# Threshold attention and hash-routed experts: moving GpSimd's scatters and early gathers between the steps of a head pair, and thinning the copies behind the experts' transfers

## The chip, the core and the metric

The kernel runs on one core of a Trainium2 chip. The metric is the device time of one execution in microseconds (us), the median of three runs. A core has five engines that run their own instruction queues side by side and wait for each other through semaphores: TensorE (PE, matrix products and transposes), VectorE (DVE), ScalarE (ACT), GpSimd (POOL) and SyncE (SP, which here only issues DMA transfers). GpSimd issues the indirect transfers, those in which a list of indices says which rows go where.

## The reference

Two blocks follow each other. The first is attention with a threshold: 8 batches, 8 heads, 576 tokens, head size 64, in float32.

```python
scores = scale * np.matmul(q, k.transpose(0, 1, 3, 2))
thresh = np.max(scores, axis=-1, keepdims=True) - tau
scores = np.where(scores >= thresh, scores, -1000000000.0)
scores = scores - np.max(scores, axis=-1, keepdims=True)
attn = np.exp(scores)
attn = attn / (np.sum(attn, axis=-1, keepdims=True) + 1e-09)
return np.matmul(attn, v).astype(np.float32)
```

Its output, brought to 4608 rows of 512 numbers, goes through one of 8 experts for each row. A hash of the token's id picks the expert.

```python
expert_idx = token_ids * np.int64(2654435761) % np.int64(E)
for e in range(E):
    mask = expert_idx == e
    xe = x[mask]
    h = np.maximum(xe @ w1[e], 0.0)
    out[mask] = h @ w2[e]
```

w1 takes a row from 512 to 1024 numbers, w2 back to 512.

## The kernel before

**Attention** is cut into 32 head pairs p: two heads of one batch, and the batch runs fastest, so that pairs 8·hp to 8·hp + 7 belong to heads 2·hp and 2·hp + 1. A pair has five steps, numbered s = 0 to 4. Step 0 takes the last 64 queries of both heads together; steps 1 to 4 take 128 queries of each head. The loop counts steps through with n = 5p + s, from 0 to 165, and LAST = 160 is the first step past the last pair. The order of all instructions in this loop is written out by hand, and each engine executes its own in this order.

One step's work passes through the engines like this:

- `score` (L235, PE) writes the scores of the next step into PSUM, in a buffer `sc`.
- `negate` (L246, DVE) copies them out negated, as `ns`, and keeps the row's extreme. After the last head of the step GpSimd adds the threshold to it (L253, `thr`).
- `expo` (L260, ACT) takes the exponential into `w`.
- `mask` (L271, DVE), one step later, sets what lies under the threshold to zero, for which it needs `thr`, and sums the row.
- `turn_w` (L282, PE), two steps later, transposes the weights into a PSUM buffer `tr`. There is one such buffer. `put_wT` (L298 and L303, ACT) copies it out to `wT_a` or `wT_b`, and only then can the next transposes begin.
- `av_part` (L313, PE) multiplies the transposed weights with v. `put_oT` (L329, ACT) copies the products out, `turn_o` (L282, PE, written to `av`) transposes them back.
- `add_eps` (L343, GpSimd, in step 1 of the next pair) and the reciprocal (L740, DVE, in step 2, ahead of that step's negations) prepare the divisor `rec` from the row sums.
- `put_xm` (L352, DVE, in step 0 two pairs later) divides, and SyncE stores the result to `x_scratch` in DRAM: one transfer at L358 and two at L363.
- `scale_k` (L215, GpSimd) scales the keys of the next pair, in step 1.

**Routing** goes on beside this, in small pieces. The tokens' slots are computed early. Then `scatters` gives one piece a call: 36 times an indirect transfer of 128 token numbers to the table of slots (L542), then some empty pieces, then the loads of the table into `sidx`, `stok` and `stok_odd`, and at last the indices of the first expert's rows, `gidx_0`. The loop takes one piece at the end of each of the steps 0, 2, 3 and 4.

**Early gathers**: of the first expert's rows 5 times 128 are needed, each in four parts of 128 columns (one part for each of the four groups of heads). Three of the four parts are complete before attention ends, so 15 pieces can be fetched in it: `fetch_early` (gather at L119 from `x_scratch` into `xg`) fetches one of them if n is over G0 and pieces are left. It is called at the start of each step 0 and at the end of each of the steps 3 and 4; with G0 = 130 the first is at n = 133 and the last at n = 155, which is step 0 of pair 31. All gathers read the tensor to which `put_xm` writes.

**The experts** follow, each with rows gathered (`fetch`, L119), transposed, multiplied with w1 and w2 and scattered to the output (`put_squares`, L1042). While one expert is multiplied, the rows of another come in and those of a third go out. Behind each of these indirect transfers stands `pause`, which copies one index table over another that is no longer used (L1027, 128 partitions by 152 numbers), twice; this takes place 157 times in the kernel: behind the 127 scatters of `put_squares` for the experts but the last and behind the 30 gathers of `fetch` for the experts from 2 on. The scatters of the last expert have no `pause`.

Of the kernel before, what the change touches and what calls it, by code (L numbers as in the profile page):

```python
# [20 lines left out]
def kernel(  # L21
# [12 lines left out]
    nc = tc.nc  # L34

    B, H, D, S = qT.shape
    N, DIN = out.shape
    E, _, F = w1.shape
    P = 128
    HP = H // 2  # L40
# [10 lines left out]
    NS = 5  # L51
# [47 lines left out]
    stok = consts.tile([P, E, NB], I32, name="stok")  # L99
    stok_odd = consts.tile([P, E, NB], I32, name="stok_odd")  # L100
# [23 lines left out]
    def fetch_0(kt, hp):  # L124
        gather(x_rows, xg_bufs[kt][:, P * hp:P * hp + P], gidx_0[:, kt, hp:hp + 1])
# [18 lines left out]
    with tc.tile_pool(name="a_q", bufs=1) as a_q, \  # L144
# [73 lines left out]
        def heads(n):  # L218
            return 1 if n % NS == 0 else 2
# [317 lines left out]
        placed, routed = [], []  # L537
# [130 lines left out]


        LAST = NS * NP  # L670
        G0 = NS * ((HP - 1) * B + 2)
        early = [(kt, hp) for kt in range(KT) for hp in range(HP - 1)]
        pieces, scatter_pieces = route(), scatters()
        h_pieces, held, LATE = early_h(), {}, (0, 6, 1, 7, 2, 3, 4, 5)
# [2 lines left out]
        def fetch_early(n):  # L677


            if n > G0 and early:  # L680
                assert routed
                fetch_0(*early.pop(0))

        def fill(n):
            for _ in range(n):
                next(h_pieces, None)

        with tc.manual_schedule():
            make_identity(nc, ident[:])

            tr = ps_tr.tile([P, 2, 512], FP32, name="tr")
            for _ in range(17):
                nc.tensor.transpose(tr[:, 0, 0:P], ident[:], ident[:])
            nc.gpsimd.dma_start(out=tau_in[:],
                                in_=bass.AP(tensor=tau.tensor, offset=0, ap=[[0, P], [1, 1]]))

            nc.vector.tensor_scalar(out=k_scale[:], in0=tau_in[:], scalar1=0.0, scalar2=SCALE,
                                    op0=ALU.is_ge, op1=ALU.mult)  # L700
            nc.vector.tensor_scalar(out=kts[0][:, 0], in0=kts[0][:, 0], scalar1=k_scale[:],
                                    scalar2=None, op0=ALU.mult)
            nc.scalar.activation(kts[0][:, 1], kts[0][:, 1], AF.Copy, scale=k_scale[:])
            nc.vector.tensor_scalar(out=drop[:], in0=tau_in[:], scalar1=0.0, scalar2=3e38,
                                    op0=ALU.is_lt, op1=ALU.mult)
            nc.vector.tensor_tensor(out=drop[:], in0=drop[:], in1=tau_in[:], op=ALU.max)
            constants()
            next(pieces)
            score(0, 0)
            for n in range(LAST + NS + 1):  # L710
                p, s = divmod(n, NS)
                m = n - 2
                if s == 0:
                    fetch_early(n)
                if s == 0 and p + 2 < NP:
                    load_pair(p + 2)
                if s == 0 and p + 1 < NP:
                    load_v(p + 1)
                if s == 2 and p in (20, 24):
                    load_w1(p // 4 - 5)  # L720
                if s == 2 and p in (22, 26):
                    load_w2((p - 22) // 4)

                if (s == 3 and p > 0 or s == 2 and p in (9, 11, 13)) and not placed:
                    next(pieces)
                if s == 1 and 3 <= p < 2 + KT:
                    nc.sync.dma_start(out=xg_bufs[p - 2][:], in_=xg_bufs[0][:])

                if s == 1 and 2 + KT <= p < 2 + KT + N // DIN:
                    r0 = DIN * (p - 2 - KT)  # L730
                    nc.sync.dma_start(
                        out=x_dram[r0:r0 + DIN, DIN - P:].rearrange("(t p) m -> p t m", p=P),
                        in_=xg_bufs[0][:].rearrange("p (t m) -> p t m", m=P))
                q = p - 1
                if s == 1 and 0 <= q < NP:
                    add_eps(q)
                if s == (1 if p else 3) and p + 1 < NP:
                    scale_k(p + 1)
                if s == 2 and 0 <= q < NP:
                    nc.vector.reciprocal(recs[q][:], recs[q][:])  # L740
                if n == LAST + NS:
                    fill(2)
                if s == 0 and p >= 2:
                    turn_o()
                if n == LAST:
                    for k in (0, 2):
                        tr = ps_sc.tile([P, 2, 512], FP32, name="sc")
                        early_xT(tr, k, k + 2, 0, CO - 1)
                if s in (1, 2) and 0 <= q < NP and n != LAST + 1:
                    av_part(q, 0, ((0, 1, 2), (3, 4))[s - 1])  # L750
                if n < LAST and s in (1, 2):
                    negate(n, 0)
                    expo(n, 0)
                if s == 2 and 0 <= q < NP:
                    put_oT(0)
                if n > LAST:
                    fill(1)
                turned = 0 <= m < LAST
                if turned:
                    tr = turn_w(m, 0)  # L760
                    put_wT(m, 0, tr)
                if n == LAST:
                    put_xm(p - 2)
                    av_part(q, 0, (0, 1, 2))
                if n >= LAST:
                    fill(1)
                if n == LAST:
                    tr = ps_sc.tile([P, 2, 512], FP32, name="sc")
                    early_xT(tr, 4, 5, 0, CO - 1)
                if s in (3, 4) and 0 <= q < NP:  # L770
                    av_part(q, 1, ((0, 1, 2), (3, 4))[s - 3])
                if n < LAST and s not in (1, 2):
                    negate(n, 0)
                    expo(n, 0)
                if s == 0 and p > 0 and not placed:
                    next(pieces)
                if s == 0 and p >= 2 and n != LAST:
                    put_xm(p - 2)
                if s == 4 and 0 <= q < NP:
                    put_oT(1)  # L780
                if s in (3, 4) and turned:
                    tr = turn_w(m, 1)
                if n + 1 < LAST:
                    score(n + 1, 0)
                if s == 4 and turned:
                    put_wT(m, 1, tr)
                if n < LAST and heads(n) == 2:
                    negate(n, 1)
                    expo(n, 1)
                if s == 3 and turned:  # L790
                    put_wT(m, 1, tr)
                if n + 1 < LAST:
                    score(n + 1, 1)
                if s in (0, 1) and turned:
                    tr = turn_w(m, 1)
                    put_wT(m, 1, tr)
                if 0 < n <= LAST:
                    for j in range(heads(n - 1)):
                        mask(n - 1, j)
                if s != 1 and placed:  # L800
                    next(scatter_pieces, None)
                if s > 2:
                    fetch_early(n)
                if n == LAST:
                    fill(1)
            assert not early
            nc.vector.tensor_tensor(out=stok[:], in0=stok[:], in1=stok_odd[:], op=ALU.min)
            for h in range(4):
                rows, n = slice(32 * h, 32 * h + 32), (NB - h + 3) // 4
                nc.vector.tensor_copy(gidx[rows, 0:n], stok[rows, E - 1, h::4])  # L810
                nc.vector.tensor_copy(gidx[rows, KT - 1:KT],
                                      stok[rows, E - 1, NB - 4 + h:NB - 3 + h])
            for g in range(4):
                rows, n = slice(32 * g, 32 * g + 32), min(KT, NB - KT * g)
                nc.vector.tensor_copy(gidx_x[rows, 1:, 0:n], stok[rows, 1:, KT * g:KT * g + n])
            for _ in pieces:
                pass
            nc.vector.scalar_tensor_tensor(
                out=qidx[:], in0=stok[:], scalar=4.0,
                in1=quart[:, :, None].to_broadcast([P, E, NB]), op0=ALU.mult, op1=ALU.add)  # L820
            for kt in range(KT):
                fetch_0(kt, HP - 1)
            fill(FO * 2 * (CO - 1) - 18)
            tr = ps_tr.tile([P, 2, 512], FP32, name="tr")
            early_xT(tr, 0, KT, CO - 1, CO)

    with tc.tile_pool(name="m_x", bufs=1) as m_x, \
# [195 lines left out]

        def pause():

            for _ in range(2):
                nc.gpsimd.tensor_copy(stok_odd[:], stok[:])  # L1027

        def put_squares(e, i):

# [174 lines left out]
```

## Time and profile before

| what | us |
|---|---|
| median of three runs (lowest, highest) | 918.26 (918.19, 919.33) |
| the profiled execution | 926.27 |
| its span, first to last instruction | 924.6 |
| GpSimd: thr, L253, x160, mean | 0.652 |
| GpSimd: scatter, L542, x36, mean | 1.247 |
| GpSimd: early gather, L119 with gidx, x20, mean | 1.247 |
| GpSimd: rec addition, L343, x64, mean | 0.235 |
| GpSimd: copy of `pause`, L1027, x314, mean | 0.445 |
| GpSimd: scatter of the experts, L1042, x127, mean | 1.100 |

The x20 early gathers are the 15 of the loop and five for the last part. The scatters run from 196.5 to about 320 us, the early gathers from 383.9 to 449.5, and the experts from about 470 us to the end.

The profile's first part gives for each engine the time in which it executed, with its share of the span and its number of instructions. The view by windows gives the same for stretches of the span: behind the stretch's length each engine's busy time. The chain of waits follows the work back from a point in time: at each step to what released it, or to the instruction ahead of it on its engine. Its lines are start, length and what. The timeline gives every instruction with start, length, engine, line, operation, output and input; in brackets stands how long the engine was idle before it and what ended the idle time. The records of PE are modelled at their ends, and spans on GpSimd are rough.

### The profile page before, as it was taken

What the parts mean: (1) busy time and instruction counts of PE and PEld (TensorE: products, weight loads), DVE (VectorE), ACT (ScalarE), POOL (GpSimd) and SP (SyncE); (2) the same over time, 40 slices, a digit from 0 to 9 for tenths busy, and PEclk for the clock granted to TensorE, in tenths of its full rate; (3) what the DMA queues carried; (4) which work ended last, traced back from release to release, by engine and by line L of the source; (5) the groups of instructions that cost most, each with busy time, mean ns of one, the idle gap of its engine ahead of it and who ended that gap; (6) DMA issues with size and microseconds to landing.
All of it is one profiled execution on the core that took longest, in us unless ns stands there. A gap on an engine that the chain in (4) does not pass through costs nothing.

```text
span 924.6 us, 21039 instructions
## 1 busy us (share of the span) xinstructions
PE 906.9 (98%) x7495; PEld 661.6 (72%) x7495; DVE 759.9 (82%) x1654; ACT 457.3 (49%) x741; POOL 550.1 (59%) x842
## 2 busy tenths in 40 slices
PE   7999999999999999999999999999999999999997
PEld 4666666656666666565668879788887978879785
DVE  8999999999999999999945696867768685786741
ACT  6888888888888898788922020110202011020210
POOL 4233432456666623446414588787787877878773
PEclk9999999999999999999999999999999999999999
DMA  7454463554545668734011636445252543522001
GB/s 175 95 146 123 107 152 96 134 134 101 124 100 149 167 164 220 209 96 108 16 33 56 195 118 185 136 125 196 63 199 90 170 155 90 218 61 67 28 28 62
DMA packets 114777, 113.13 MB, mean 122 GB/s; under 512 B 32475, under 2 KB 89315, under 8 KB 114672
## 3 DMA queue, kind: packets, MB, share of 16 engines
q1 hardware_dynamic: 105168, 92.64, 37.0%
q0 software_dynamic: 9072, 18.91, 6.6%
q8 instruction: 61, 1.00, 0.4%
q14 instruction: 44, 0.36, 0.1%
q10 hardware_dynamic: 432, 0.21, 0.1%
HBM read 81.99 MB, written 21.44 MB: 112 GB/s over the span
## 4 chain that ended last, share of the span: by engine, by line
PE 83%; POOL 6%; issue 4%; DVE 3%; ACT 2%; DMA 1%; SPq 0%; POOLq 0%; DVEq 0%; ACTq 0%
PE bank L941 18%; PE av L313 18%; PE sc L941 18%; PE sc L235 14%; PE tr L282 11%; POOL out_dram L1042 4%; PE sc L640 3%; POOL stok_odd L1027 2%; PE av L282 1%; DVE ns L246 1%; DVE w L271 1%; ACT w L260 1%; DMA k_sb<-in_k_dram 1%; ACT wT_b L303 1%; PE bank L658 0%
## 5 line engine op out<-in xcount | busy, mean ns | idle before, releaser
L260 ACT ACTIVATE w<-ns,nmx 128x576 f32<-128x576 f32 x288 | 220.4, 776 | 28.6 <-DVE ns L246 27.9
L271 DVE SCALAR_TENSOR_TENSOR w<-ns,thr,w 128x576 f32<-128x576 f32 x288 | 225.7, 816 | 0.0
L253 POOL TENSOR_SCALAR thr<-nmx,drop 128x2 f32<-128x2 f32 (+1 forms) x160 | 104.4, 652 | 188.9 <-DVE ns L246 179.1
L246 DVE TENSOR_SCALAR_CACHE_REDUCE ns<-sc 128x576 f32<-128x576 f32 x288 | 205.7, 746 | 8.5 <-PE sc L235 7.7
L235 PE MATMUL sc<-k_sb,q 64*128 64x288 f32 (+1 forms) x1280 | 178.2, 422 | 1.1 <-DVE ns L246 0.6
L282 PEld LDWEIGHTS tr<-ident,w 64*128 64x128 f32 x2624 | 105.6, 138 | 96.9 <-ACT wT_b L303 35.3
L1042 POOL DMA_INDIRECT out_dram<-o_q,qidx x127 | 139.7, 1100 | 57.8 <-issue 49.2
L282 PE MATMUL tr<-ident,w 64*128 64x64 f32 x2624 | 139.2, 230 | 7.7 <-ACT wT_b L303 4.8
L1027 POOL COPY stok_odd<-stok 128x152 int32<-128x152 int32 x314 | 139.9, 445 | 10.0
L948 ACT ACTIVATE h<-h 128x576 f32<-128x576 f32 (+1 forms) x56 | 38.8, 693 | 142.8 <-DVE h L861 142.0
L235 PEld LDWEIGHTS sc<-k_sb,q 64*128 64x128 f32 (+1 forms) x1280 | 92.2, 177 | 23.5 <-DVE ns L246 9.8
L313 PE MATMUL av<-wT_a,v 128*64 128x320 f32 (+1 forms) x704 | 100.4, 418 | 0.2
L303 ACT COPY wT_a<-tr 128x512 f32<-128x512 f32 (+1 forms) x128 | 81.7, 638 | 20.6 <-PE tr L282 20.1
L303 ACT COPY wT_b<-tr 128x512 f32<-128x512 f32 (+1 forms) x128 | 81.3, 635 | 18.2 <-PE tr L282 10.2
L313 PE MATMUL av<-wT_b,v 128*64 128x256 f32 x640 | 83.2, 389 | 0.0
L313 PEld LDWEIGHTS av<-wT_a,v 128*64 128x64 f32 x704 | 43.7, 136 | 29.0 <-DVE xm L352 0.7
L951 ACT COPY p<-bank 128x576 f32<-128x576 f32 (+2 forms) x11 | 7.0, 634 | 107.5 <-PE bank L941 102.5
L313 PEld LDWEIGHTS av<-wT_b,v 128*64 128x64 f32 x640 | 40.2, 136 | 18.8 <-issue 0.7
L119 POOL DMA_INDIRECT xg<-x_scratch,gidx_x x35 | 41.8, 1193 | 19.2 <-issue 9.3
L542 POOL DMA_INDIRECT slot_scratch<-tok,slot_i x36 | 44.9, 1247 | 9.5 <-issue 7.6
L951 ACT COPY p<-sc 128x576 f32<-128x576 f32 (+2 forms) x11 | 7.0, 637 | 84.7 <-PE sc L941 79.8
L941 PE MATMUL bank<-h,w_sb 128*128 128x288 f32 (+3 forms) x192 | 48.1, 404 | 0.0
(198 smaller groups left out, 1402.4 us busy)
## 6 DMA issues: line engine op xcount, KB each, us to landing
w_sb<-in_moe_w_dram SPq DMA_DIRECT2D x16, 2048.0 KB
q<-in_q_dram SPq DMA_DIRECT2D x62, 288.0 KB
v<-in_v_dram SPq DMA_DIRECT2D x32, 256.0 KB
x_scratch<-xm SPq DMA_DIRECT2D x32, 256.0 KB
xT<-xq SPq DMA_DIRECT2D x84, 80.0 KB
k_sb<-in_k_dram SPq DMA_DIRECT2D x31, 144.0 KB
k_sb<-in_k_dram SPq DMA_DIRECT2D x32, 112.0 KB
x_scratch<-xg SPq DMA_DIRECT2D x9, 256.0 KB
```

The source lines that it names most:

```text
L235: nc.tensor.matmul(sc[out_rows, i, 0:S2], lhsT=q_sb[rows, h, q0:q1], rhs=k_sb[rows, h], start=True, stop=True)
L246: nc.vector.tensor_scalar(out=ns[:].rearrange("p (i s) -> p i s", i=2), in0=sc[:, :, 0:S2], scalar1=-1.0, scalar2=None, op0=ALU.mult, op1= ...
L253: nc.gpsimd.tensor_scalar(out=thr[:, 0:j + 1], in0=stats[n][0][:, 0:j + 1], scalar1=drop[:], scalar2=None, op0=ALU.add)
L260: nc.scalar.activation(w, nss[n, j][:], AF.Exp, bias=stats[n][0][:, j:j + 1], scale=-1.0)
L271: nc.vector.scalar_tensor_tensor(out=w, in0=nss.pop((n, j))[:], scalar=stats[n][1][:, j:j + 1], in1=w, op0=ALU.is_le, op1=ALU.mult, accum_ ...
L282: nc.tensor.transpose(dst[:, r, 64 * c:64 * c + 64], src[rows, c0:c0 + P], ident[rows, rows])
L303: nc.scalar.copy(dst, tr[:, :, 0:64 * n_c].rearrange("p r (c q) -> p r c q", c=n_c))
L313: nc.tensor.matmul(av[64 * j:64 * j + 64, g, c0:c1], lhsT=v_sb[:, c, 64 * j:64 * j + 64], rhs=wT[g][:, i, c0:c1], start=(c == 0), stop=stop)
L542: nc.gpsimd.indirect_dma_start(out=slot_dram[c % 2][:, :], out_offset=bass.IndirectOffsetOnAxis(ap=slot_i[:, c:c + 1], axis=0), in_=tok[:, ...
L941: nc.tensor.matmul(ps[:, i, 0:width], lhsT=lhsT, rhs=y[:, c], start=c == 0, stop=c == n_k - 1)
L1027: nc.gpsimd.tensor_copy(stok_odd[:], stok[:])
L1042: inst = nc.gpsimd.indirect_dma_start(out=rows[:, :], out_offset=bass.IndirectOffsetOnAxis(ap=idx, axis=0), in_=o_sb, in_offset=None, boun ...
```

## The change

Four edits. One piece of `scatters` is taken at the end of each of the steps 0, 1, 2 and 3. The early gathers are called at the ends of the steps 2 and 3 alone, and G0 is 125, so that the first is at n = 127; twelve are fetched in this way up to n = 153. What is left then, three, is fetched at the end of step n = 155 (LAST − NS), one after another. And `pause` copies once.

```diff
         LAST = NS * NP
-        G0 = NS * ((HP - 1) * B + 2)
+        G0 = NS * ((HP - 1) * B + 1)
@@
                 m = n - 2
-                if s == 0:
-                    fetch_early(n)
                 if s == 0 and p + 2 < NP:
                     load_pair(p + 2)
@@
                 if 0 < n <= LAST:
                     for j in range(heads(n - 1)):
                         mask(n - 1, j)
-                if s != 1 and placed:
+                if s < NS - 1 and placed:
                     next(scatter_pieces, None)
-                if s > 2:
+                if s in (2, 3):
                     fetch_early(n)
+                if n == LAST - NS:
+                    while early:
+                        fetch_early(n)
                 if n == LAST:
                     fill(1)
@@
         def pause():
 
-            for _ in range(2):
-                nc.gpsimd.tensor_copy(stok_odd[:], stok[:])
+            nc.gpsimd.tensor_copy(stok_odd[:], stok[:])
```

The number of scatters and gathers and their data stay the same. In the program built from it, PE, ACT, SyncE and DVE have their instructions in the same order as before. On GpSimd the scatters stand behind the thr of steps 0, 1, 2 and 3 and the gathers behind those of steps 2 and 3. At n = 155 GpSimd has the thr of that step, the three gathers, and then the rec additions and thr of the next step; the first of the three gathers waits for the three stores of `x_scratch` that the same step issues.

## The prediction
> **What bounds the kernel now.** I read four views in this order: busy time by engine, engine time by stage, the chain of waits, and the timeline of single engines where two pairs of heads differ. The first two:
> ```profile
> PE 906.9 (98%) x7495; PEld 661.6 (72%) x7495; DVE 759.9 (82%) x1654; ACT 457.3 (49%) x741; POOL 550.1 (59%) x842
> ...
> core 0: us, PE busy (x) PEld busy (x) DVE busy (x) ACT busy (x) POOL busy (x), PEclk, DMA share, GB/s
> 200.00:300.00 100.00, 98.74 (x1219) 60.98 (x1216) 96.54 (x267) 85.98 (x140) 66.02 (x85) 1.00 0.50 121
> 333.50:375.00 41.50, 41.50 (x524) 26.29 (x522) 41.11 (x117) 36.66 (x61) 13.23 (x24) 1.00 0.65 161
> 375.00:450.00 75.00, 71.59 (x882) 44.59 (x880) 70.45 (x193) 61.87 (x102) 42.20 (x55) 1.00 0.48 124
> 480.00:886.00 406.00, 406.00 (x1667) 341.38 (x1666) 297.78 (x356) 55.85 (x87) 312.73 (x457) 1.00 0.40 123
> ```
> TensorE (PE) sets the time. In the experts (480 to 886 us) it is busy for all of 406.00 us. In attention it is full where GpSimd (POOL) issues no indirect transfer (333.5 to 375) and falls short by 1.26 us of 100 beside the scatters and by 3.41 of 75 beside the early gathers. So only what gives PE time in attention, or takes it, moves the end.
>
> How large the loss is comes from the chain of waits (start, length, what). I take the x12 product that opens step 1 of a pair as the mark, once per pair of heads. Two of these pairs, a clean one and one with gathers:
> ```profile
> 373.20 0.46 PE av L282 x10
> 373.66 0.25 PE tr L282 x8
> 373.91 1.03 PE sc L235 x8
> 374.94 0.31 PE tr L282 x10
> 375.25 1.76 PE av L313 x12
> ...
> 387.10 0.46 PE av L282 x10
> 387.56 0.36 PE tr L282 x8
> 387.93 1.95 PE sc L235 x8
> 389.87 0.02 issue
> 389.89 0.59 ACT wT_b L303
> 390.49 0.05 issue
> 390.53 0.52 PE tr L282 x10
> 391.06 1.76 PE av L313 x12
> ```
> From the first scores' start to the mark the clean pair needs 375.25 − 373.91 = 1.34 us, the other 391.06 − 387.93 = 3.13. The second transposes of step 0 wait for the only `tr` buffer, which ScalarE's copy wT_b frees, and that copy is late. The timeline of GpSimd and ScalarE says why:
> ```profile
> 388.43 1.02 POOL L119 DMA_INDIRECT xg<-x_scratch,gidx  x1 [0.30 <-issue]
> ...
> 389.89 0.58 ACT L303 COPY wT_b<-tr 128x512 f32<-128x512 f32 x1 [1.81 <-PE sc L235]
> ...
> 390.53 0.52 PE L282 MATMUL tr<-ident,w 64*128 64x64 f32 x10 [1.58 <-ACT wT_b L303]
> ```
> The copy starts 0.44 us after the gather of step 0 ends (389.45). Beside a scatter it is the same at a smaller size: the last scatter of step 4 ran 273.90 to 275.20, and the copy began at 275.38, 0.32 us after ScalarE fell idle. In clean pairs the copy follows the activation before it with no idle time.
>
> Over whole pairs, by the marks: clean 361.36 to 375.25 is 13.89 us. Nine scatter pairs (190.13 to 319.64) take 129.51, which is 129.51 − 9 x 13.89 = 4.50 over. Five gather pairs (375.25 to 449.49 by the chain) take 74.24, 74.24 − 69.45 = 4.79 over. Scatters at the ends of steps 2 and 3 show no PE wait behind them; only an indirect transfer issued at the end of step 4 or the start of step 0 does.
>
> [...] The trace shows a late PE-to-ACT handover of 0.3 to 1.9 us beside GpSimd transfers[...]; I know no mechanism for it. [...] here a gather was issued at 448.54 and the store that had to wait for it left SyncE at 450.89, 2.35 us later.
>
> **The change part by part.** All sums are against the profiled execution (926.27 us, span 924.6); it stands 926.27 − 918.26 = 8.0 us over the median of the runs, and I carry the difference over unchanged.
>
> (a) Scatters at the ends of steps 0, 1, 2, 3 instead of 0, 2, 3, 4. Number and data stay (36, mean 1.25 us, row L542). Removing the one at step 4 takes away what made the copy late: up to −4.50 us. Here I take −4.5, that is, step 0's scatter stays harmless as it is now and the one at step 1 is harmless too. It lands behind step 1's thr, where GpSimd idles 1.44 us before step 2's thr (281.26 in the pair of 276.54), so that thr moves by at most 0.1 us; its masks run a step later. If the cover fails, the same late handover hits step 1's transposes: price in the first rival. Bounds of the part: 0 to −4.5, and +7.7 on the bad side.
>
> (b) Gathers at the ends of steps 2 and 3 from pair 25 on, instead of at 3, 4 and 0 from pair 26 on: twelve there, by the same argument −4.8 us (bounds 0 and −4.8). The first pair's step 2 gather follows that pair's xm store by more closely and may wait some 1.4 us; DVE has about 2 us until it needs the next thr, so nothing. The stores of xm, which now wait 28.4 us in all on SyncE for gathers in flight, are freed; no PE work waits for them, so nothing there either.
>
> (c) The three remaining gathers sit together in step 0 of pair 31, behind that step's xm and its three stores, and in GpSimd's order ahead of the rec additions and thr of step 1. In that order they wait for the stores. What stands there now:
> ```profile
> 447.96 0.82 DVE L352 TENSOR_TENSOR xm<-av,rec 128x640 f32<-128x640 f32 x1
> ...
> 450.50 0.54 POOL L343 TENSOR_SCALAR rec<-rs 128x9 f32<-128x9 f32 x2
> ...
> 452.27 0.21 DVE L740 RECIPROCAL rec<-rec 128x10 f32<-128x10 f32 x1
> ```
> xm ends at 448.78. Its stores, no longer behind a gather, leave at once and land about 3 us later (estimate, from stores of the earlier steps that landed 1.8 us after the last issue and 2.8 after the first), near 451.9. Three gathers of 1.0 to 1.4 us with 0.3 us between them: 4.0 to 4.5, so to about 456.2. rec takes 0.54, and the reciprocal, now at 452.27, comes near 457. DVE executes in order: its stall is 4.4 to 5.0 us, and behind it queue step 2's negations, which free the score buffers, and the masks, which feed the transposes. PE has about 0.6 us of slack there. Taken: +4.3 us (bounds +3 and +5). PE is full from then on, so nothing gives it back.
>
> (d) One copy instead of two behind 157 of the experts' transfers: 157 x 0.445 = 70 us of GpSimd time, row L1027. PE has no gap there, so 0. The timeline's last transfers have a period of 2.10 us (902.59 to 904.69) and the last of them with copies ends at 906.36, three us before the next at 909.43; that tail has no copy behind it and waits for the last products. A denser issue could collide with loads, or free a buffer sooner: −0.5 to +1.
>
> Sum: −4.5 − 4.8 + 4.3 + 0 = −5.0. Profiled 921.3; median 913.3, taken as 913.4.
>
> **Rivals.** First, slower: the scatter at step 1 does to step 1 what that of step 4 does to step 0. In its favour: step 1 also has two sets of transposes through one buffer, and I don't know the mechanism. Against: scatters at steps 2 and 3 do nothing although their transposes use the same buffer. Price: ScalarE's copy, normally about 3.8 us after the mark, would wait for the scatter's end at 4.85, and the transposes lose some 0.85 us a pair; 9 x 0.85 = 7.7, net −5.0 + 7.7 = +2.7, median 921.0. It decides for slower from (5.0 + 1.8) / 9 = 0.76 us a pair; at 0.55 the gain is gone.
>
> Second, part of the loss is moved or was only there under the profiler, while the wait in (c) stays: half of (a) and (b), −4.65 + 4.3 = −0.35, no change, 917.9; none of it, +4.3, 922.6. In favour: I can't name the mechanism. Against: every one of 14 pairs shows it, no clean pair does.
>
> Third, the wait in (c) is hidden, if the stores land sooner or DVE has more slack than I see: −9.3, median 909.0. Against it, DVE is busy for 70.45 of 75 us in that stretch.
>
> That the change doesn't do what it says is excluded for the order: PE, ACT, SyncE and DVE keep their orders in the built program, GpSimd's is as told above.
>
> **How the numbers follow.** Forecast, within 911 to 915.5: 0.47. Third rival 0.15. First rival 0.14. Half gone 0.14, none left 0.10. A measurement tells 0.2%, 1.8 us, from no change. Faster: 0.47 + 0.15 = 0.62; same 0.14; slower 0.24. The range leaves out half of the third rival and those of the slower cases beyond 920.8: 909 to 920.8.
>
> **What would show it.** Right: in the changed profile no PE wait for wT_b at step 0, marks 13.9 us apart in scatter and gather pairs; one DVE stall of 4 to 5 us before the reciprocal of pair 31, charged to GpSimd's rec, and a wait of the first of three gathers on x_scratch<-xm. (a) is wrong if PE waits for ACT in step 1 of scatter pairs; (d) if PE shows gaps after 480 us.

## The result, and the profile after

The changed kernel is slower: 923.56 us median of five executions (922.65 to 924.02) against 918.26, ratio 1.0054, 95% interval [1.0043, 1.0065], so 5.3 us. The forecast was 913.4.

The first thing to see is an oddity. The profiled execution after the change took 923.56 us with a span of 921.9, just what its timed series says. The profiled execution before took 926.27, eight more than its series. Set side by side, the two profiles show the span shrinking by 2.7 us while the times grow by 5.3. The first part of the page of the profile after, and then its windows (as before: stretch, length, busy time of PE, PEld, DVE, ACT, POOL, granted clock, DMA share, GB/s):

```profile
PE 906.3 (98%) x7495; PEld 662.7 (72%) x7495; DVE 757.9 (82%) x1654; ACT 457.2 (50%) x741; POOL 478.3 (52%) x685
```
```profile
200.00:300.00 100.00, 100.00 (x1258) 63.04 (x1254) 99.62 (x275) 88.09 (x145) 68.73 (x86) 1.00 0.53 131
...
375.00:450.00 75.00, 71.76 (x897) 45.28 (x894) 69.54 (x193) 62.77 (x103) 36.28 (x52) 1.00 0.44 115
...
480.00:886.00 406.00, 406.00 (x1670) 341.97 (x1669) 295.52 (x351) 57.25 (x88) 257.78 (x328) 1.00 0.41 125
```

The sum over the whole span tells little: TensorE is busy for 906.3 us, before for 906.9. By stretches TensorE is full beside the scatters now (100.00, it was 98.74), and full in the experts (406.00) with 55 us less work on GpSimd. Between 375 and 450 it still lacks 3.24 us, nearly as much as before (3.41), but this time in one piece. The waits of TensorE from 190 to 500 us (what waited, for what, total, times, longest) are only these:

```profile
PE sc L235 <- DVE ns L246: 3.2, 1, 3.2
PE av L282 <- ACT oT L329: 0.2, 1, 0.2
PE tr L282 <- ACT wT_a L298: 0.2, 1, 0.2
```

The waits for wT_b at step 0 are gone, and the marks stand 13.89 us apart (246.51, 260.40, 274.28 beside scatters; 385.41, 399.46, 413.35 beside gathers, 14.05 and 13.89). The one long wait is in pair 31. The timelines of SyncE, GpSimd, VectorE and TensorE there:

```profile
440.68 0.37 SPq L358 DMA_DIRECT2D x_scratch<-xm  x1
441.10 1.16 SPq L363 DMA_DIRECT2D x_scratch<-xm  x2
...
444.31 1.09 POOL L119 DMA_INDIRECT xg<-x_scratch,gidx  x1 [3.93 <-DMA x_scratch<-xm]
445.71 1.00 POOL L119 DMA_INDIRECT xg<-x_scratch,gidx  x1 [0.30 <-issue]
447.01 1.01 POOL L119 DMA_INDIRECT xg<-x_scratch,gidx  x1 [0.30 <-issue]
448.10 0.53 POOL L343 TENSOR_SCALAR rec<-rs 128x9 f32<-128x9 f32 x2
...
448.66 0.22 DVE L738 RECIPROCAL rec<-rec 128x10 f32<-128x10 f32 x1 [4.44 <-POOL rec L343]
...
449.59 1.51 PE L235 MATMUL sc<-k_sb,q 64*128 64x288 f32 x8 [3.24 <-DVE ns L246]
451.30 0.69 PE L282 MATMUL tr<-ident,w 64*128 64x64 f32 x8 [0.20 <-ACT wT_a L298]
451.92 2.63 PE L313 MATMUL av<-wT_b,v 128*64 128x256 f32 x12
```

(Line numbers from the changed kernel: its L738 is L740 of the kernel before.) Read from the top: the stores leave at once, the gathers wait for them (3.93 us), rec queues behind the gathers, the reciprocal waits 4.44 us for rec, the negations behind it (L246) free the score buffer late, and TensorE stands idle. The last line shows a second cost: the x12 product takes 2.63 us where it takes 1.52 in other pairs. The windows of the same stretch have the reason in the third column from the right, the granted clock:

```profile
448.00:450.00 2.00, 0.41 (x4) 0.30 (x4) 1.34 (x4) 0.43 (x1) 0.79 (x4) 1.00 0.02 6
450.00:452.00 2.00, 1.80 (x18) 0.89 (x16) 2.00 (x7) 1.92 (x4) 0.72 (x1) 0.70 0.03 8
452.00:454.00 2.00, 2.00 (x10) 1.16 (x12) 2.00 (x7) 1.92 (x3) 0.72 (x1) 0.50 0.00 0
454.00:456.00 2.00, 2.00 (x26) 1.16 (x24) 0.92 (x3) 0.70 (x2) 0.00 (x0) 0.94 0.00 0
```

So there were two theories to tell apart. Theory 1: the late copies of wT_b, and the 9.3 us on which the prediction's gain rested, belonged to the one execution that was profiled; the timed executions didn't have them, and the wait in pair 31 is the whole result. Theory 2: every execution of the kernel before has them, the change removed 9.3 us, and something else, the pauses for want of another, adds 9.6 on top of the wait.

### The profile page after: what moved, and what is told of

Same layout as the page of the kernel before. It is cut to its first block, busy times and chain, and to the rows that moved or that the text cites. A ratio compares the mean times of both kernels' runs of the same rounds, so it can differ in the third digit from the quotient of the medians.

```text
span 921.9 us, 20884 instructions
## 1 busy us (share of the span) xinstructions
PE 906.3 (98%) x7495; PEld 662.7 (72%) x7495; DVE 757.9 (82%) x1654; ACT 457.2 (50%) x741; POOL 478.3 (52%) x685
## 4 chain that ended last, share of the span: by engine, by line
PE 48%; POOL 25%; issue 17%; DVE 5%; ACT 2%; DMA 1%; SPq 1%; POOLq 1%; DVEq 0%; ACTq 0%
PE av L313 18%; PE sc L235 15%; POOL out_dram L1042 14%; PE tr L282 10%; POOL stok_odd L1027 8%; POOL xg L119 3%; PE sc L640 3%; PE av L282 1%; DVE ns L246 1%; DVE w L271 1%; DMA xT<-xq 1%; ACT w L260 1%; SPq L1072 0%; DVE o_q L1033 0%; DVE xq L1064 0%
## 5 line engine op out<-in xcount | busy, mean ns | idle before, releaser
L246 DVE TENSOR_SCALAR_CACHE_REDUCE ns<-sc 128x576 f32<-128x576 f32 x288 | 205.4, 745 | 5.1 <-PE sc L235 4.3
L1042 POOL DMA_INDIRECT out_dram<-o_q,qidx x127 | 133.5, 1051 | 125.3 <-DVE o_q L1033 104.1
L253 POOL TENSOR_SCALAR thr<-nmx,drop 128x2 f32<-128x2 f32 (+1 forms) x160 | 101.6, 635 | 177.3 <-DVE ns L246 168.1
L1027 POOL COPY stok_odd<-stok 128x152 int32<-128x152 int32 x157 | 77.4, 493 | 0.6
L942 PE MATMUL sc<-h,w_sb 128*128 128x288 f32 (+3 forms) x192 | 47.6, 401 | 0.0
```

What stands on the lines that cost most here:

```text
L246: nc.vector.tensor_scalar(out=ns[:].rearrange("p (i s) -> p i s", i=2), in0=sc[:, :, 0:S2], scalar1=-1.0, scalar2=None, op0=ALU.mult, op1= ...
L253: nc.gpsimd.tensor_scalar(out=thr[:, 0:j + 1], in0=stats[n][0][:, 0:j + 1], scalar1=drop[:], scalar2=None, op0=ALU.add)
L942: nc.tensor.matmul(ps[:, i, 0:width], lhsT=lhsT, rhs=y[:, c], start=c == 0, stop=c == n_k - 1)
L1042: inst = nc.gpsimd.indirect_dma_start(out=rows[:, :], out_offset=bass.IndirectOffsetOnAxis(ap=idx, axis=0), in_=o_sb, in_offset=None, boun ...
```

## The experiments

All times are medians beside runs of the kernel before on the same chip, which stood at 917.99, 918.14 and 918.11 us in the three groups.

**1. The kernel before again.** No edit.

> The kernel before, unchanged, for a second profile. Theory 1 (the late copies of wT_b, and with them 9.3 us, belong to the one execution that was profiled): timed 918.3, the profiled execution within 1.5 us of that instead of 926.3, its marks (x12 product of step 1) 13.9 us apart in scatter and gather pairs too, no PE wait for wT_b at step 0. Theory 2 (every execution has them, and the profile adds about 8 us of its own somewhere else): marks 14.4 us apart beside scatters and 14.8 beside gathers again, whatever the profiled time is.

Measured: 918.62 us, ratio 1.0002 [0.9994, 1.0011]; the profiled execution 919.2, span 917.6. TensorE has no wait at all between 190 and 450 us, and the eight pairs from the mark at 205.54 to that at 316.68 take 111.14 us, 13.89 each. Here is a pair with a gather in step 0, the chain of waits and then the timeline of GpSimd and ScalarE:

```profile
398.83 1.03 PE sc L235 x8
399.86 0.30 PE tr L282 x10
400.16 1.76 PE av L313 x12
```
```profile
398.53 1.08 POOL L119 DMA_INDIRECT xg<-x_scratch,gidx  x1 [0.16 <-issue]
398.93 0.59 ACT L303 COPY wT_b<-tr 128x512 f32<-128x512 f32 x1
```

The copy begins at 398.93, in the middle of the gather, and TensorE goes through. From the scores to the mark it is 1.33 us, where the first profile had 3.13. The gather is the same, in the same place; the late handover isn't there. The copy begins 0.10 us after the end of the transposes (398.42 + 0.41 = 398.83), while the transfer runs (398.53 to 399.61); in the first profile it began 0.41 to 2.03 us after them in the 14 pairs with such a transfer, and 0.09 to 0.59 us after the transfer had ended. Beside none of the 14 does TensorE wait here. That speaks for theory 1.

**2. The scatters alone.**

```diff
-                if s != 1 and placed:
+                if s < NS - 1 and placed:
```

> The kernel before with the scatters at steps 0, 1, 2, 3 alone. Theory 1: no loss to remove in timed executions, so 918.3, within 1 us of before. Theory 2: -4.5 us, 913.8. If step 1's scatter hurts: up to +7.7 us.

Measured: 917.82 us, ratio 0.9998 [0.9990, 1.0006]. Neither gain nor loss; the marks are 13.89 us apart (246.10, 259.99, 273.88), so the scatter at step 1 is harmless as well.

**3. The three late gathers alone.**

```diff
-                if s == 0:
+                if s == 0 and n < LAST - NS:
                     fetch_early(n)
...
-                if s > 2:
+                if s > 2 and n < LAST - NS - 2:
                     fetch_early(n)
+                if n == LAST - NS:
+                    while early:
+                        fetch_early(n)
```

> The kernel before with its last three early gathers moved to the end of step n = 155, behind that step's stores; all other gathers, the scatters and the pauses as before. Theory 1: this is the whole loss: +5 us (3.2 us of PE idle, 0.2 more behind it and 1.7 of slower products while the clock recovers), 923.4. Theory 2: +5 us on its own too, but then the -9.3 of the moved scatters and gathers needs a further +9.6 from the pauses.

Measured: 923.82 us, ratio 1.0061 [1.0048, 1.0075]. This part alone has the whole loss.

**4. The pauses alone.**

```diff
-            for _ in range(2):
-                nc.gpsimd.tensor_copy(stok_odd[:], stok[:])
+            nc.gpsimd.tensor_copy(stok_odd[:], stok[:])
```

> The kernel before with one copy in each pause. Theory 1: PE has no gap in the experts, so 918.3, within 1 us of before, with 1 us or less either way from transfers that stand closer together. Theory 2: about +9.6 us, 927.9, with PE gaps after 480 us.

Measured: 917.99 us, ratio 1.0000 [0.9991, 1.0008]. GpSimd's busy time falls to 484.6 us from 554.5 in the first experiment, and nothing follows from it. Theory 2 is out: it has the late copies in every execution, and in the first experiment's TensorE waits for none; it has the pauses cost 9.6 us, and they cost nothing. The moved gathers were not run alone; the fifth experiment has them together with the other parts.

**5 to 7. Where in the wait the cost sits.** Three places for the three gathers in the changed kernel. In the fifth they go to n = 157, 158, 159:

```diff
-                if n == LAST - NS:
-                    while early:
-                        fetch_early(n)
+                if n == LAST - 1:
+                    fetch_early(n)
```

> The changed kernel, but its last three gathers go one each to the ends of steps n = 157, 158 and 159 (pair 31, steps 2 to 4), where the stores of step 155 landed long ago. If the triple is the whole loss: 918.0, within 1 us of before. If the moved scatters, the moved gathers and the single copy cost something together that none costs alone: between 919 and 923.5.

In the sixth they stand as one block at the start of step 155, ahead of its stores:

```diff
             for n in range(LAST + NS + 1):
                 p, s = divmod(n, NS)
                 m = n - 2
+                if n == LAST - NS:
+                    while early:
+                        fetch_early(n)
...
-                if n == LAST - NS:
-                    while early:
-                        fetch_early(n)
```

> The changed kernel with the three gathers at the start of step n = 155, ahead of that step's stores, in one block. Theory S (the wait for the stores makes rec late): the gathers run from about 438.7 to 442.8, rec is done by 443.6, before DVE comes to its reciprocal at about 444.2; 918.3, within 1 us of before. Theory G (three gathers in a row ahead of rec are enough, whatever they wait for): 921 to 923.5.

In the seventh they stand one step later, behind rec and one more thr:

```diff
-                if n == LAST - NS:
+                if n == LAST - NS + 1:
```

> The changed kernel with the three gathers one step later, at the end of n = 156: rec and step 156's thr are then ahead of them in GpSimd's order, and behind them stands step 157's thr, which DVE needs about 3 us after the gathers end their wait. Theory S with rec as the instruction that matters: at most +0.5 us, 918.0 to 918.8. If the three gathers near the stores cost PE in another way: +3 us or more, 921 or above.

Measured: 918.48 (ratio 1.0006 [0.9998, 1.0014]), 918.28 (1.0002 [0.9994, 1.0010]) and 918.38 us (1.0004 [0.9995, 1.0012]). All three are the time of before. In the sixth GpSimd executes

```profile
439.86 1.37 POOL L119 DMA_INDIRECT xg<-x_scratch,gidx  x1 [0.17 <-issue]
441.53 1.01 POOL L119 DMA_INDIRECT xg<-x_scratch,gidx  x1 [0.30 <-issue]
442.84 1.26 POOL L119 DMA_INDIRECT xg<-x_scratch,gidx  x1 [0.31 <-issue]
444.14 0.31 POOL L253 TENSOR_SCALAR thr<-nmx,drop 128x1 f32<-128x1 f32 x1
444.54 0.88 POOL L343 TENSOR_SCALAR rec<-rs 128x9 f32<-128x9 f32 x2
```

The same three gathers in the same step, begun without waiting, leave rec done 3.27 us after the mark (442.15), which is in time; in the changed kernel it is done 7.58 after it (448.63 − 441.05). Three gathers in a row, ahead of rec, are not enough for a cost. What costs is that they begin only when the stores have landed, while rec stands behind them.

**8. The clock.** TensorE gets something to do in the gap:

```diff
                     tr = turn_w(m, 0)
+                    if n == LAST - NS + 2:
+                        for _ in range(28):
+                            nc.tensor.transpose(tr[:, 1, 384:512], ident[:], ident[:])
                     put_wT(m, 0, tr)
```

> The changed kernel with 28 transposes of the identity[...] put on TensorE between the transposes and the scores of step 157, where it stands idle for 3.24 us; they write a part of the PSUM tile that nobody reads. If the 1.7 us of slower products behind the gap come from the clock that drops after an idle stretch: 921.8, the clock 1.00 in every 1 us stretch, the x12 product 1.5 us instead of 2.63. If they come from elsewhere: 923.5, as the changed kernel.

Measured: 922.34 us, ratio 1.0053 [1.0041, 1.0065]; single executions from 921.82 to 925.73, so the time alone doesn't separate it from the changed kernel's 923.56. The profile does:

```profile
450.00:452.00 2.00, 1.72 (x20) 1.04 (x20) 2.00 (x7) 2.00 (x5) 0.73 (x1) 1.00 0.00 0
452.00:454.00 2.00, 2.00 (x28) 1.28 (x22) 2.00 (x7) 2.00 (x4) 0.72 (x1) 1.00 0.00 0
```
```profile
451.36 1.52 PE L313 MATMUL av<-wT_b,v 128*64 128x256 f32 x12
```

The added transposes run from 445.93 to 449.21, and the scores behind them come no later than in the changed kernel (8.56 us after the mark, there 8.54). The clock stays at 1.00 and the x12 product takes 1.52 us again. What the low clock costs is in the table below: 1.3 us, not the 1.7 that I had expected.

**9. A single execution of the kernel before.** No edit; the question was whether a lone profiled execution brings the late copies back.

> The kernel before, unchanged, once more as a single execution with a profile and no timed series around it. If late copies of wT_b come with such a single execution: about 926, marks 14.4 us apart beside scatters. If they belong to that one execution: 918 to 919.5, marks 13.9 us apart.

Measured: 918.58 us, marks 13.89 us apart beside scatters (246.62, 260.52, 274.40). In this one execution they did not come.

**10 and 11. The dose.** One, then two of the three gathers behind the stores of step 155, the others in steps 3 and 4 of pair 31. The tenth:

```diff
-                if s in (2, 3):
+                if s in (2, 3) and n != LAST - 3:
+                    fetch_early(n)
+                if n in (LAST - NS, LAST - 1):
                     fetch_early(n)
-                if n == LAST - NS:
-                    while early:
-                        fetch_early(n)
```

> The changed kernel with one of the three gathers left behind the stores of step 155, and the other two at the ends of n = 158 and 159. The gather would end at about 445.4, rec at 446.0, DVE stalls 1.8 us instead of 4.4, TensorE 2.6 us less than the 3.4 it lost by waiting: +0.8 us, 919.0, with no drop of the clock.

The eleventh:

```diff
-                if s in (2, 3):
+                if s in (2, 3) and n != LAST - 3:
                     fetch_early(n)
                 if n == LAST - NS:
-                    while early:
-                        fetch_early(n)
+                    fetch_early(n)
+                    fetch_early(n)
```

> The changed kernel with two of the three gathers behind the stores of step 155 and the third at the end of n = 158. DVE stalls 3.1 us, TensorE waits 2.1: +2.3 us, 920.4, if the clock holds over a gap of 2.1 us; +3.6, 921.7, if it drops as behind the gap of 3.2.

Measured: 919.55 (1.0016 [1.0008, 1.0024]) and 922.12 us (1.0046 [1.0032, 1.0060]). The reciprocal waited 1.83 and 3.14 us in the profiles, as expected; TensorE lost 0.7 more in the tenth than I had worked out. In the eleventh TensorE waits for the negations as before, only shorter:

```profile
447.27 0.22 DVE L738 RECIPROCAL rec<-rec 128x10 f32<-128x10 f32 x1 [3.14 <-POOL rec L343]
448.20 1.43 PE L235 MATMUL sc<-k_sb,q 64*128 64x288 f32 x8 [1.94 <-DVE ns L246]
```

**12. rec ahead of the gathers.**

```diff
-                if s == 1 and 0 <= q < NP:
+                if s == 1 and 0 <= q < NP and n != LAST - NS + 1:
                     add_eps(q)
...
                 if n == LAST - NS:
+                    add_eps(q)
                     while early:
                         fetch_early(n)
```

> The changed kernel with the rec additions of pair 30 put ahead of the three gathers in GpSimd's order; the gathers stay behind the stores of step 155. If rec alone is what the wait delays to the cost of TensorE: 918.3. If the next thr behind the gathers counts as well: thr of step 156 would end at about 447.9 where its mask is due at about 445.8, DVE stalls some 2 us one place later, and TensorE loses 0.5 to 2: 919 to 920.5.

Measured: 921.32 us, 1.0037 [1.0023, 1.0051]. Freeing rec isn't enough. The wait has moved one instruction on:

```profile
447.65 0.59 POOL L253 TENSOR_SCALAR thr<-nmx,drop 128x2 f32<-128x2 f32 x2
448.01 0.82 DVE L271 SCALAR_TENSOR_TENSOR w<-ns,thr,w 128x576 f32<-128x576 f32 x1 [2.80 <-POOL thr L253]
448.98 0.46 PE L282 MATMUL tr<-ident,w 64*128 64x64 f32 x8 [2.04 <-DVE w L271]
```

thr of step 156 was next in the queue behind the gathers; the mask waits 2.80 us for it, and the transposes 2.04 for the mask. In the seventh experiment, where this thr also stood ahead and the first gather had nothing to wait for, the mask waited 0.5 us for the thr after it, and the time shows nothing of it.

**What TensorE lost, in one measure.** In each profile I take the time from the mark in pair 31 to the first of the 64 products with w1 behind attention (L640). It is 27.34 us in the first experiment (441.92 to 469.26) and 32.78 after the change (441.05 to 473.83). The two lines of each, the first experiment's first:

```profile
441.92 1.84 PE L313 MATMUL av<-wT_a,v 128*64 128x320 f32 x12
469.26 15.17 PE L640 MATMUL sc<-xT,w_sb 128*128 128x272 f32 x64
...
441.05 1.84 PE L313 MATMUL av<-wT_a,v 128*64 128x320 f32 x12
473.83 15.17 PE L640 MATMUL sc<-xT,w_sb 128*128 128x272 f32 x64
```

| kernel (experiment) | wait of the reciprocal (in 12 the mask) in pair 31, us | mark to products, us | over experiment 1, us | timed, over before, us |
|---|---|---|---|---|
| before (1) | 0 | 27.34 | | +0.6 |
| changed | 4.44 | 32.78 | 5.44 | +5.3 |
| three gathers alone (3) | 4.4 | 32.89 | 5.55 | +5.8 |
| three spread (5) | 0 | 27.33 | 0.0 | +0.3 |
| gap filled (8) | 4.5 | 31.47 | 4.13 | +4.2 |
| one gather (10) | 1.83 | 28.83 | 1.49 | +1.4 |
| two gathers (11) | 3.14 | 30.16 | 2.82 | +4.0 |
| rec first (12) | 2.80 | 29.76 | 2.42 | +3.2 |

One stretch of 27 us holds the changed kernel's whole loss. From one gather to two the loss grows by 1.33, the gather itself with its gap being 1.40 (444.22 to 445.62 in the eleventh). From two to three it grows by 2.62: 1.31 for the gather, and another 1.31 (5.44 − 4.13 by the filled gap) for the clock, which in the profile of the eleventh was 1.00 in each window of 1 us from 446 to 456, behind a wait of 1.94 us. Its timed median is 1.2 above what the profiled execution's stretch accounts for. A drop of the clock in its other executions would fit. They have no trace, but every execution has its mean granted clock on record. The profiled executions of the changed kernel and of the third experiment, in which the x12 product behind the gap takes 2.63 and 2.76 us, have 0.996, and so low a mean can come from elsewhere: that of the first experiment has 0.995 without the gap (its eight score products at 18.06 us took 2.19 us, those at 13.41 took 1.26, and its page gives the last fortieth of the span a clock of 8 tenths). The profiled executions of the eighth, tenth, eleventh and twelfth, with 1.00 in the windows behind the gap, have 0.998, 0.998, 0.998 and 0.999. The four others of the eleventh (921.99 to 922.84 us; the profiled one took 920.75) have 0.996 twice and 0.997 twice. By this, as an estimate, two had a stretch of low clock somewhere and two may have had one. Whether it stood behind this gap no trace shows, so it stays open, and with it the 0.8 us that the twelfth's median lies above its stretch.

No version is faster than the kernel before: the lowest median, 917.82 in the second experiment, is that of before within its interval.

## Why the prediction was wrong

- **What bounds the kernel** was read rightly in kind: TensorE sets the time, and only its gaps in attention count. The two gaps that carried the numbers, 4.50 us beside scatters and 4.79 beside gathers, were true of the profiled execution and of no other that was traced: five more profiles of kernels with indirect transfers at step 4 or the start of step 0 (experiments 1, 3, 4 and 9, of which 1 and 9 are the kernel before itself, and 2 for its gathers) show none. A small part of the two numbers was never a loss: the nine and five pairs that took 129.51 and 74.24 us take 125.45 and 69.76 in experiment 1, so the first profile lost 8.54 us there, not 9.29.
- **The step that failed** is the sentence "it stands 926.27 − 918.26 = 8.0 us over the median of the runs, and I carry the difference over unchanged". The difference was not a constant of profiling: experiment 1's profiled execution took 919.2. It was nearly the sum that I then took off as gain, 4.50 + 4.79 = 9.3, so (a) and (b) took from the median a loss that the median never held. Without (a) and (b) the sum reads +4.3, and the median 922.6, which the second rival had as "none of it" with a chance of 0.10.
- **(a), scatters:** forecast −4.5, measured 0. That the scatter at step 1 is harmless was right, and the first rival (+7.7) fell with it.
- **(b), gathers at steps 2 and 3:** forecast −4.8. They were not run without the other edits; with the scatters and the pauses changed and the three gathers spread, all is 0 within [0.9998, 1.0014].
- **(c), three gathers behind the stores:** the mechanism came as told, down to the charge to rec. DVE's stall was 4.44 us (forecast 4.4 to 5.0), the stores landed 2.8 us after the first of them left (440.68 to 443.48; forecast 3), the gathers took 3.71 (4.0 to 4.5). The size was short: +4.3 against 5.44. Late scores make 3.40 of it (8.54 us from the mark to the scores of step 158, against 5.14); TensorE's slack was 4.44 − 3.40 = 1.04 us, not 0.6. The low clock makes 1.31, and the prediction has no term for it. The remaining 0.7 is the restart, for which it has none either: the scores come out slower (1.43 us for 1.19 in the tenth profile, at full clock) and the transposes wait for ScalarE (0.28 us there), which starts late as well: it is busy for 0.30 us of 446 to 447. The tenth has the same 0.7 (1.49 − 0.78).
- **The clock** has no term in the prediction, and the profile it was made from shows no drop to price: there the windows of 1 us stand at 1.00 up to 920 us, past TensorE's last product (917.71). The profile after shows the depth and length of the drop: by the windows above, the clock was at 0.50 for some 3.4 us (1.2 us of the stretch from 450, since 0.30 x 2 / 0.5 = 1.2; the whole stretch from 452; 0.2 us of that from 454). It came behind a gap of 3.24 us, when TensorE had been at work again for 1.2.
- **(d), the pauses:** forecast 0, measured 0.

What remains unexplained is why the first profiled execution had late handovers from TensorE to ScalarE beside GpSimd's indirect transfers, 14 pairs out of 14. It didn't come back in any later profile, so its cause stays open. How often it happens is open too: all timed executions of the kernel before lie between 917.39 and 919.87 us; one of the eighth experiment's six, 925.73, was long as well, and has no trace.

## What to carry to other kernels

Before a gain is summed from a profile, compare the profiled execution with the timed ones: where it is longer by more than its own overhead around the span (here 926.27 − 924.6 = 1.7 us), the loss that looks worth removing may be what made this execution longer, and a second profile of the unchanged kernel costs less than a wrong change. An instruction that waits costs what is queued behind it (here 4.44 us of the reciprocal, in the twelfth experiment 2.80 of the mask): place a transfer that must wait for a store behind everything that another engine needs soon, and count the next instruction too, not only the first. And a gap on TensorE can cost more than its length: here one of 0.6 us cost 1.5, and one of 3.24 us cost 5.4.

## What was not expected of the hardware

The clock of TensorE fell to half some 1.2 us after work had resumed (products resumed at 449.59, the clock was 1.00 until 450.8 and 0.50 from there to 454.2 by windows of 0.25 us), not in the gap itself, and cost 1.31 us on top. How long the clock outlasts the work isn't the same throughout these traces. In this gap it fell 4.5 us after the product ahead had ended (446.35 to 450.8). Behind TensorE's last product it fell after 5.3 us in the profile before (917.71; the clock of 922.75 to 923.00 is 0.97, that of 923.00 to 923.25 0.50) and after 3.6 us in the profile after (914.82; the clock of 918.25 to 918.50 is 0.88, that of 918.50 to 918.75 0.50). It held at 1.00 behind gaps of 0.63, 1.94 and 2.04 us (experiments 10, 11 and 12) and fell behind the one of 3.24; from what length on it falls was not shown. And one execution of an unchanged program, the profile before, was 8.0 us longer than the median of the others (926.27 against 918.26), with handovers from TensorE to ScalarE 0.3 to 1.9 us late, each coming within 0.6 us behind the end of an indirect transfer of GpSimd.
